# Three attention stages on one TensorE queue: the AV of one chunk and the last QK group of a later chunk moved into one slot

## The chip, the cores and the metric

One of the eight cores of a Trainium2 chip runs the kernel. The metric is the device time of one launch in microseconds, the median of several runs. Before the change it is 1178.77 us (three runs, 1178.74 to 1179.63).

Engine names as the profile has them: PE is the matrix engine (PEld its weight loads), DVE the vector engine, ACT the scalar engine, POOL GpSimd, SP the engine that only issues DMAs here.

## The reference, cut to what matters

Talking-heads attention over 4 batches, 12 heads, 448 positions, head size 64, and behind it two feed-forward stages over the 1792 tokens. All in float32.

```
scores = scale * (q @ k^T)                       # QK, per head
scores = einsum('bhij,hg->bgij', scores, w_pre)  # "pre": mixes the 12 heads
attn   = exp(scores - max) / (sum + 1e-9)
attn   = einsum('bhij,hg->bgij', attn, w_post)   # "post": mixes the heads again
x      = attn @ v                                # AV, per head
x = moe_solu(x)    # 768 -> 1024 -> 768, softmax gate and layer norm
x = moe_relu2(x)   # 768 -> 2048 -> 768, squared relu
```

## The kernel before, in words

Each batch's 448 query rows are cut into four **chunks** of 120, 120, 120 and 88 rows, sixteen chunks in all. A chunk is worked in **blocks** of up to ten query rows times twelve heads (120 partitions): twelve blocks in a chunk of 120 rows, nine in one of 88. There are 180 blocks. `ch["first"]` is a chunk's first block and `nb` its number of blocks.

The work of a chunk, in the order in which data flows:

- `qk(c, g)`, three groups g of four heads each. A group makes four PSUM tiles of 120x448; the two halves of a pair of heads lie in partitions 0 to 63 and 64 to 127 of the inputs and are issued in turn (line 199). From chunk 2 on each product is three matmuls of split numbers, so a group is 12 matmuls of 64 rows. ACT copies the four tiles to `ssrc` (line 208).
- `shuffle(t)`, a DMA on SP that regroups one block's rows with all heads into `sdst` (line 214; seven buffers).
- `pre(t)` (line 226, the full 120x120 weights), `negmax` on DVE (239), `expo` on ACT (251), `weigh` for a pair of blocks (DVE 260 and 262, then POOL 268, for the last 14 blocks ACT 275), `post(t)` (line 288), `post_out` on DVE (302).
- `av(c, p)`, six head pairs (line 315). Each is 8 products with weights of 112x64, one head in output partitions 0 to 63, the other in 64 to 127. ACT copies each tile out to `xt` (lines 325, 330). In the trace each float32 product of pre, post and AV shows as two matmuls, so a chunk's AV is 96 of them.

QK and AV tiles come from one PSUM ring, `psq_p` with tag "qa" and four buffers. After the last QK group that pool is closed and AV goes on with a ring of two (line 582).

**What sets the order.** There is no scheduler: every engine runs the program in the order in which the code issues it, and that order is a list of slots written out by hand. Slot s issues `pre(s+3)` and `post(s)`, and between them the jobs entered for that slot with `at_slot`: QK groups, splits of q and k into two parts (DVE and POOL), AV. Line 554 sets the order of the kinds inside a slot. For a chunk c behind a chunk of 12 blocks, `first` of the chunk between being F, the QK groups of c stand in slots F-8, F-4 and F; AV of chunk c-2 stands in slot F+2. The first shuffle of chunk c stands in slot F+4.

Pieces of the first feed-forward stage's weights are converted on the side: `filler` hands out one step of `narrow` (ACT line 70, DVE lines 71 to 83) at a time, about one piece per three slots up to slot 150. From slot `last_raw` (155) on, `prep_first` loads that stage's weights and inputs (`wraw`, SP lines 393 and 402; casts on DVE and ACT, line 406; POOL line 407): one step per slot up to slot `last_qk`, the slot of the last QK group, and two per slot from there (lines 584 to 588). `last_qk` is also where the QK pools are closed.

Of the kernel before, what the change touches and what calls it, by code (L numbers as in the profile page):

```python
# [18 lines left out]
def kernel(  # L19
# [69 lines left out]
    def filler():  # L89

        for q in (fill2, fill):
            while q:
                if next(q[0], None) is None:
                    q.pop(0)
                else:
                    break
# [24 lines left out]
    for b in range(B):  # L121
        for (i0, n) in CHUNKS:
            c, nb, oa = len(chunks), -(-n // R), 0
# [86 lines left out]
    def shuffle(t):  # L210
        c, k, r, oa = blocks[t]
        n, nb = chunks[c]["n"], chunks[c]["nb"]
        d = late_p.tile([120, S], F32, tag="sdst", name="sdst", bufs=7)
        nc.sync.dma_start(out=d[0:r * H], in_=ssrc[c][k:k + (r - 1) * nb + 1:nb])
        sdst[t] = d
# [6 lines left out]
    def pre(t):  # L222
        m = blocks[t][2] * H
        d = sdst.pop(t)
        ps = psb_p.tile([128, 512], F32, tag="pre", name="ps_pre", bufs=2)
        nc.tensor.matmul(  # L226
            out=ps[0:m, 0:S],
            lhsT=wpre_bd[0:m].rearrange("p i g -> p (i g)")[:, 0:m],
            rhs=d[0:m],
            start=True,  # L230
            stop=True,
        )
        pres[t] = ps

    def negmax(t):
        ps = pres[t]
        m = blocks[t][2] * H
        nm = late_p.tile([120, 1], F32, tag="nm", name="nm", bufs=4)
        nc.vector.tensor_reduce(out=nm[0:m], in_=ps[0:m, 0:S], op=ALU.max, axis=AX.X, negate=True)  # L239
        pres[t] = (ps, nm)  # L240

    def expo(t):
        m = blocks[t][2] * H
        ps, nm = pres.pop(t)
        e = late_p.tile([120, S], F32, tag="e", name="e", bufs=4)
        if t % 2 == 0:
            sms[t] = late_p.tile([120, 2], F32, tag="sm", name="sm", bufs=4)
            if m < 120 or blocks[t + 1][2] < R:
                nc.vector.memset(sms[t], 1.0)
        sm = sms[t - t % 2][:, t % 2:t % 2 + 1]  # L250
        nc.scalar.activation(  # L251
            out=e[0:m], in_=ps[0:m, 0:S], func=AF.Exp, bias=nm[0:m], scale=1.0, accum_out=sm[0:m]
        )
        es[t] = e

    def weigh(t):

        m = max(blocks[u][2] for u in (t, t + 1)) * H
        sm = sms.pop(t)
        nc.vector.tensor_scalar(out=sm[0:m], in0=sm[0:m], scalar1=1e-9, scalar2=None, op0=ALU.add)  # L260
        filler()
        nc.vector.reciprocal(sm[0:m], sm[0:m])  # L262
        filler()
        for u in (0, 1):
            m = blocks[t + u][2] * H
            w = late_p.tile([120, H, R], F32, tag="w", name="w", bufs=4)
            if t < tail:
                nc.gpsimd.tensor_tensor(  # L268
                    out=w[0:m].rearrange("p g i -> p (g i)"),
                    in0=wpost_bd[0:m].rearrange("p g i -> p (g i)"),  # L270
                    in1=sm[0:m, u:u + 1].to_broadcast([m, H * R]),
                    op=ALU.mult,
                )
            else:
                nc.scalar.activation(out=w[0:m], in_=wpost_bd[0:m], func=AF.Copy, scale=sm[0:m, u:u + 1])  # L275
            ws[t + u] = w
# [5 lines left out]
    def post(t):  # L282
        r = blocks[t][2]
        m = r * H
        e, w = es.pop(t), ws.pop(t)
        ps = psa_p.tile([JW, NJ, H, R], F32, tag="post", name="ps_post", bufs=2)
        for j in range(NJ):
            nc.tensor.matmul(  # L288
                out=ps[:, j, :, 0:r],
                lhsT=e[0:m, j * JW:(j + 1) * JW],  # L290
                rhs=w[0:m, :, 0:r],
                start=True,
                stop=True,
            )
        pps[t] = ps

    def post_out(t):
        c, k, r, oa = blocks[t]
        ps = pps.pop(t)
        if c not in at:  # L300
            at[c] = late_p.tile([JW, NJ, H, 120], F32, tag="at", name="at", bufs=2)
        nc.vector.tensor_copy(at[c][:, :, :, oa:oa + r], ps[:, :, :, 0:r])  # L302
# [109 lines left out]
    def h1(m):  # L412
        t = xs.pop(m)
        pool = psi_p if m % 2 else psh_p
        ps = pool.tile([128, 2, 512], F32, tag="h", name="ps_h")
        for cc in range(CC):
            for (a, w) in ((0, 0), (0, 1), (1, 0)):
                for u in range(2):
                    nc.tensor.matmul(  # L419
                        out=ps[:, u],  # L420
                        lhsT=t[:, a, cc],
                        rhs=w1i[cc][:, w, u * 512:(u + 1) * 512],
                        start=(cc == 0 and a == 0 and w == 0),
                        stop=(cc == CC - 1 and a == 1),
                    )
            yield True
        hps[m] = ps

    def run(part):
        for _ in part:  # L430
            pass
# [54 lines left out]
    def at_slot(s, f, *a):  # L486
        jobs.setdefault(s, []).append((f, a))

    NG = HP // KG
    splits = []  # L490
    for c, ch in enumerate(chunks):
        if c:
            p = chunks[c - 1]
            beg = ch["first"] - DS - p["nb"]
            if c > 1:
                splits += [(beg - 2, split_q, c, u) for u in (1, 0)]
            for g in range(NG):
                s = beg + (g * p["nb"]) // NG
                at_slot(s, qk, c, g)
                if c > 1 and (ch["i0"] == 0 or c == 2):  # L500
                    splits += [(s - 2, split_k, ch["b"], g, u) for u in (1, 0)]

    s = NB
    for by, f, x, *a in sorted(splits, key=lambda j: -j[0]):
        s = min(s, by - by % 2)
# [24 lines left out]
    for s in range(lo_s, NB + 12):  # L530
        js = jobs.pop(s, [])
        for kind in (load_k, load_q, load_v, load_w1, load_const):
            for f, a in js:
                if f is kind:
                    f(*a)
        if 0 <= s + DS < NB:
            shuffle(s + DS)
        for f, a in js:
            if f is store_w1:
                f(*a)  # L540
            elif f is x_out and s < NB:
                f(*a)
        if 0 <= s + DP < NB:
            pre(s + DP)
        if 0 <= s - 1 < NB:
            post_out(s - 1)
        if 0 <= s + 1 < NB and (s + 1) % 2 == 0:
            weigh(s + 1)
        else:
            filler()  # L550
        if 0 <= s + DP < NB:
            negmax(s + DP)
            expo(s + DP)
        for kind in (qk, split_q, split_k, av):
            for f, a in js:
                if f is kind:
                    f(*a)
        for f, a in js:
            if f is start_w1:
                f(*a)  # L560
        if 0 <= s < NB:
            post(s)
        filler()
        if s >= NB:
            for f, a in js:
                if f is x_out:
                    f(*a, nc.scalar)
        if s == last_raw:
            raws.__exit__(None, None, None)
            wi1 = tc.tile_pool(name="wi1", bufs=1, side="left", reuse_waits="tile")  # L570
            wi1_p = wi1.__enter__()
            prep = prep_first()
        if s == last_qk:
            early.__exit__(None, None, None)
            sspools[0].__exit__(None, None, None)
            wi1b = tc.tile_pool(name="wi1b", bufs=1, side="left", reuse_waits="tile")
            wi1b_p = wi1b.__enter__()
            psq.__exit__(None, None, None)
            psh = tc.tile_pool(name="psh", bufs=1, side="left", space=PSUM, reuse_waits="tile")
            psh_p = psh.__enter__()  # L580
            pst = tc.tile_pool(name="pst", bufs=1, side="left", space=PSUM, reuse_waits="tile")
            av_ring[:] = [pst.__enter__(), "av", 2]
            h10 = h1(0)
        if last_raw < s <= min(last_qk, last_raw + 7):
            next(prep)
        if s > last_qk:
            next(prep, None)
            next(prep, None)
        if s in (170, 172, 176, 177):
            next(h10)  # L590
        if s == NB:
            run(prep)
            run(h10)
# [388 lines left out]
```

## Time and profile before

| | |
|---|---|
| median of three runs | 1178.77 us |
| span of the profiled execution | 1178.6 us (the page gives no other time for it) |
| PE busy | 1168.5 us, 99% of the span |
| DVE, ACT, POOL busy | 744.8, 490.9, 279.8 us |
| granted PE clock | 9 of 9 in each of the 40 slices |
| attention stage | 0 to about 466 us |

A matmul's busy time in this profile overlaps that of the next, and its end is modelled. The reading used below is therefore the distance between the starts of two groups of matmuls in the timeline, which holds whatever PE did or waited for in between.

### The profile page before, as it was taken

Reading aid. Unit: us, or ns where it says so; the run is one execution under the profiler, and the core shown is the slowest. Engines: PE = TensorE matmul, PEld = TensorE weight load, DVE = VectorE, ACT = ScalarE, POOL = GpSimd, SP = SyncE. Lnnn points to the kernel's source line nnn. Section 1 sums busy time; section 2 is a strip of 40 time slices with the busy share of each in tenths; the row PEclk is TensorE's granted clock in tenths of the full one; section 3 lists DMA queues with packets and bytes.
Section 4 is the critical chain, followed back from the end, with each engine's and each line's share of the span. In section 5 each row is a group of like instructions: output and inputs, shape, how many; then the busy total and the mean of one; then the engine's idle time right before and its main releaser. Section 6 shows DMA issues by size and latency. Waiting matters only on the chain.

```text
span 1178.6 us, 21505 instructions
## 1 busy us (share of the span) xinstructions
PE 1168.5 (99%) x8034; PEld 1021.1 (87%) x8034; DVE 744.8 (63%) x1480; ACT 490.9 (42%) x1206; POOL 279.8 (24%) x386
## 2 busy tenths in 40 slices
PE   9999999999999999999999999999999999999998
PEld 4777777777777768899899999999999999999998
DVE  4776777677777664853354378457676767676734
ACT  4556555666666554422122146533232222222211
POOL 2342223223322161730110074211111111111100
PEclk9999999999999999999999999999999999999999
DMA  6875766566656452411110265212121212121113
GB/s 178 215 200 166 224 185 193 164 216 202 185 179 195 137 172 86 121 48 48 54 41 27 70 200 173 69 41 64 45 62 46 65 44 63 45 66 43 41 68 121
DMA packets 103267, 134.40 MB, mean 114 GB/s; under 512 B 21499, under 2 KB 86395, under 8 KB 103163
## 3 DMA queue, kind: packets, MB, share of 16 engines
q1 hardware_dynamic: 102379, 132.75, 37.7%
q8 instruction: 64, 1.05, 0.4%
q14 instruction: 40, 0.33, 0.1%
q10 hardware_dynamic: 784, 0.27, 0.1%
HBM read 71.65 MB, written 22.81 MB: 80 GB/s over the span
## 4 chain that ended last, share of the span: by engine, by line
PE 91%; DVE 2%; DMA 2%; ACT 1%; issue 1%; POOL 1%; SPq 0%; POOLq 0%; DVEq 0%; ACTq 0%
PE ps_y L885 19%; PE ps_h L846 19%; PE ps_post L288 12%; PE ps_pre L226 10%; PE ps_h L419 10%; PE ps_o L692 8%; PE ps_av L315 6%; PE ps_qk L199 6%; PE ps_tr L678 1%; DMA x2r<-x2D 1%; DMA wraw<-w1iD 1%; DMA wr<-in_moe_w_out_dram 1%; DVE nm L239 1%; DVE at L302 0%; ACT e L251 0%
## 5 line engine op out<-in xcount | busy, mean ns | idle before, releaser
L846 PE MATMUL ps_h<-x,ti 128*128 128x384 f32 (+1 forms) x1440 | 241.6, 325 | 0.0
L885 PE MATMUL ps_y<-to,g 128*128 128x384 f32 x1332 | 239.3, 336 | 1.1 <-ACT y L894 1.1
L846 PEld LDWEIGHTS ps_h<-x,ti 128*128 128x128 f32 x1440 | 236.6, 188 | 0.0
L885 PEld LDWEIGHTS ps_y<-to,g 128*128 128x128 f32 x1332 | 231.0, 188 | 3.4 <-DVE y L896 1.9
L288 PEld LDWEIGHTS ps_post<-w,e 120*112 120x112 f32 (+1 forms) x1440 | 168.3, 177 | 68.4 <-issue 48.2
L302 DVE COPY at<-ps_post 112x480 f32<-112x480 f32 x180 | 117.3, 652 | 109.4 <-PE ps_post L288 108.9
L288 PE MATMUL ps_post<-w,e 120*112 120x120 f32 (+1 forms) x1440 | 182.7, 270 | 2.6 <-ACT w L275 2.1
L251 ACT ACTIVATE e<-ps_pre,nm 120x448 f32<-120x448 f32 x180 | 114.6, 637 | 132.0 <-POOL w L268 73.3
L226 PE MATMUL ps_pre<-sdst,wpre_bd 120*120 120x448 f32 x360 | 166.3, 545 | 0.8 <-ACT e L251 0.7
L854 ACT ACTIVATE r<-ps_h 128x384 f32<-128x384 f32 (+1 forms) x80 | 37.4, 468 | 213.1 <-PE ps_h L846 213.1
L692 PE MATMUL ps_o<-zt,w1o 128*128 128x384 f32 (+1 forms) x720 | 120.1, 326 | 0.0
L419 PE MATMUL ps_h<-w1i,xs 128*128 128x512 f32 x504 | 119.2, 393 | 0.4 <-ACT xt L330 0.4
L855 DVE SCALAR_TENSOR_TENSOR r<-ps_h,r 128x384 f32<-128x384 f32 (+1 forms) x80 | 42.4, 531 | 121.7 <-ACT r L854 121.7
L692 PEld LDWEIGHTS ps_o<-zt,w1o 128*128 128x128 f32 x720 | 117.0, 189 | 0.0
L239 DVE TENSOR_REDUCE nm<-ps_pre 120x1 f32<-120x448 f32 x180 | 110.2, 613 | 7.9 <-PE ps_pre L226 5.3
L896 DVE TENSOR_TENSOR y<-ps_y,y 128x768 f32<-128x768 f32 x97 | 92.4, 953 | 31.2 <-PE ps_y L885 31.2
L419 PEld LDWEIGHTS ps_h<-w1i,xs 128*128 128x128 f32 x504 | 93.9, 188 | 19.9 <-ACT xt L330 0.6
L268 POOL TENSOR_TENSOR w<-wpost_bd,sm 120x120 f32<-120x120 f32 x166 | 64.1, 406 | 188.1 <-DVE sm L262 176.8
L208 ACT COPY ssrc<-ps_qk 120x448 f32<-120x448 f32 (+1 forms) x186 | 84.9, 543 | 10.0 <-PE ps_qk L199 10.0
L315 PEld LDWEIGHTS ps_av<-at,v 112*64 112x64 f32 x1536 | 73.8, 137 | 11.4 <-ACT ssrc L208 5.3
L802 POOL TENSOR_TENSOR ti<-wt,ti 128x384 fp32r<-128x384 f32 x32 | 34.7, 1085 | 205.4 <-ACT ti L801 205.3
L315 PE MATMUL ps_av<-at,v 112*64 112x120 f32 (+1 forms) x1536 | 78.0, 261 | 0.4 <-ACT xt L325 0.3
(79 smaller groups left out, 1168.1 us busy)
## 6 DMA issues: line engine op xcount, KB each, us to landing
sdst<-ssrc SPq DMA_DIRECT2D x172, 210.0 KB
wr<-in_moe_w_in_dram SPq DMA_DIRECT2D x32, 384.0 KB
wr<-in_moe_w_out_dram SPq DMA_DIRECT2D x32, 384.0 KB
w1raw<-in_moe_w_in_dram SPq DMA_DIRECT2D x24, 256.0 KB
w1raw<-in_moe_w_out_dram SPq DMA_DIRECT2D x24, 256.0 KB
kraw<-in_kT_dram SPq DMA_DIRECT2D x24, 224.0 KB
v<-in_v_dram SPq DMA_DIRECT2D x16, 336.0 KB
out_dram<-y SPq DMA_DIRECT2D x13, 384.0 KB
```

Of the source, the lines that this page charges most:

```text
L208: (nc.vector.tensor_copy if dve else nc.scalar.copy)(ssrc[c][0:n, h, :], ps[0:n, 0:S])
L226: nc.tensor.matmul(out=ps[0:m, 0:S], lhsT=wpre_bd[0:m].rearrange("p i g -> p (i g)")[:, 0:m], rhs=d[0:m], start=True, stop=True,)
L239: nc.vector.tensor_reduce(out=nm[0:m], in_=ps[0:m, 0:S], op=ALU.max, axis=AX.X, negate=True)
L251: nc.scalar.activation(out=e[0:m], in_=ps[0:m, 0:S], func=AF.Exp, bias=nm[0:m], scale=1.0, accum_out=sm[0:m])
L288: nc.tensor.matmul(out=ps[:, j, :, 0:r], lhsT=e[0:m, j * JW:(j + 1) * JW], rhs=w[0:m, :, 0:r], start=True, stop=True,)
L302: nc.vector.tensor_copy(at[c][:, :, :, oa:oa + r], ps[:, :, :, 0:r])
L315: nc.tensor.matmul(out=ps[64 * e:64 * e + 64, 0:n], lhsT=vv[ch["b"], j][:, 2 * p + e], rhs=a[:, j, 2 * p + e, 0:n], start=(j == 0), stop=( ...
L419: nc.tensor.matmul(out=ps[:, u], lhsT=t[:, a, cc], rhs=w1i[cc][:, w, u * 512:(u + 1) * 512], start=(cc == 0 and a == 0 and w == 0), stop=( ...
L692: nc.tensor.matmul(out=ps[:, 0:width], lhsT=w1o[k][:, w, cc * 128:(cc + 1) * 128], rhs=zT[:, a, k, 0:width], start=(k == 0 and i == 0), st ...
L846: nc.tensor.matmul(out=ps[:, 0:n], lhsT=ti[:, w, cc, f * 128:(f + 1) * 128], rhs=x2[q][:, a, cc], start=(cc == 0 and i == 0), stop=(cc == ...
L885: nc.tensor.matmul(out=ps[:, u - us[0], 0:DM // 2], lhsT=g[:, a, f, o:o + 128], rhs=to[:, w, f, u * (DM // 2):(u + 1) * (DM // 2)], start= ...
L896: nc.vector.tensor_tensor(out=yo, in0=po, in1=yo, op=ALU.add)
```

## The change

QK groups of chunks from 2 on move two slots later where the chunk between has 12 blocks, so from F-8, F-4, F to F-6, F-2, F+2. The last then shares slot F+2 with AV of chunk c-2, and the order of kinds inside a slot puts AV ahead of QK. Chunks behind a chunk of nine blocks (4, 8 and 12) keep their slots.

```diff
-            for g in range(NG):
-                s = beg + (g * p["nb"]) // NG
+            shift = 2 if c > 1 and p["nb"] == 12 else 0
+            for g in range(NG):
+                s = beg + shift + (g * p["nb"]) // NG
+                if shift and g == NG - 1:
+                    s = ch["first"] - p["nb"] + 2
                 at_slot(s, qk, c, g)
                 if c > 1 and (ch["i0"] == 0 or c == 2):
                     splits += [(s - 2, split_k, ch["b"], g, u) for u in (1, 0)]
...
-        for kind in (qk, split_q, split_k, av):
+        for kind in (av, qk, split_q, split_k):
```

The first place is PE's queue around block 12, where chunk 2's last QK group and chunk 0's AV stand (`ps_qk` is QK, `ps_av` AV, `ps_pre` and `ps_post` the two mixes). Before:

```order
L226 MATMUL ps_pre<-sdst,wpre_bd 120x448
L199 MATMUL ps_qk<-k,q 120x448 x12
L288 MATMUL ps_post<-w,e 112x120 x4
L226 MATMUL ps_pre<-sdst,wpre_bd 120x448
L288 MATMUL ps_post<-w,e 112x120 x4
L226 MATMUL ps_pre<-sdst,wpre_bd 120x448
L315 MATMUL ps_av<-at,v 64x120 x48
L288 MATMUL ps_post<-w,e 112x120 x4
```

And now:

```order
L288 MATMUL ps_post<-w,e 112x120 x4
L226 MATMUL ps_pre<-sdst,wpre_bd 120x448
L315 MATMUL ps_av<-at,v 64x120 x48
L199 MATMUL ps_qk<-k,q 120x448 x12
L288 MATMUL ps_post<-w,e 112x120 x4
L226 MATMUL ps_pre<-sdst,wpre_bd 120x448
```

AV and the QK group now follow each other with no post and pre between. This happens at 11 of the 16 AVs (chunks 0, 1, 3, 4, 5, 7, 8, 9, 11, 12 and 13).

The second place is SP's queue at the start (`qraw` is the load of a chunk's queries, in two halves; `sdst` a shuffle). Before:

```order
L451 DMA wp_raw<-in_w_post_dram 120x1x12
L166 DMA qraw<-in_qT_dram 64x720 x2
L214 DMA sdst<-ssrc 120x1x448 x2
L166 DMA qraw<-in_qT_dram 64x720 x2
L214 DMA sdst<-ssrc 120x1x448 x8
```

And now:

```order
L451 DMA wp_raw<-in_w_post_dram 120x1x12
L166 DMA qraw<-in_qT_dram 64x720 x4
L214 DMA sdst<-ssrc 120x1x448 x10
L434 DMA g_sb<-in_moe_g_ln_dram 128x8x1
L214 DMA sdst<-ssrc 120x1x448 x4
```

The later K splits of chunk 2 push its query load, and the split of its queries, ahead of the first two shuffles.

The third place is SP's queue around slots 161 to 165, the last QK group and behind it (`wraw` is a step of `prep_first`). Before:

```order
L393 DMA wraw<-w1iD 128x256 x2
L214 DMA sdst<-ssrc 120x1x448
L402 DMA wraw<-xD 128x2x128 x2
L214 DMA sdst<-ssrc 120x1x448
L402 DMA wraw<-xD 128x2x128
L393 DMA wraw<-w1iD 128x256
L214 DMA sdst<-ssrc 120x1x448
L340 DMA xD<-xt 128x6x120
L393 DMA wraw<-w1iD 128x256 x2
```

And now:

```order
L393 DMA wraw<-w1iD 128x256 x2
L214 DMA sdst<-ssrc 120x1x448
L402 DMA wraw<-xD 128x2x128 x2
L214 DMA sdst<-ssrc 120x1x448
L340 DMA xD<-xt 128x6x120
L402 DMA wraw<-xD 128x2x128
L393 DMA wraw<-w1iD 128x256
```

`last_qk` goes from 159 to 161, so two steps of `prep_first` fall out of slots 160 and 161 and everything behind them comes one slot later; `xD<-xt` (AV of chunk 13) stays in slot 164.

## Rows read from the trace of the kernel before

**Rows 1.** The page: busy us (share of the span) and instructions of each engine.

```profile
PE   1168.5 (99%) x8034; PEld 1021.1 (87%) x8034; DVE 744.8 (63%) x1480; ACT 490.9 (42%) x1206; POOL 279.8 (24%) x386
```

**Rows 2.** The page: the chain of waits that ended last, by engine.

```profile
PE 91%; DVE 2%; DMA 2%; ACT 1%; issue 1%; POOL 1%; SPq 0%; POOLq 0%; DVEq 0%; ACTq 0%
```

**Rows 3.** Timeline of PE around one QK group; first start us, then us.

```profile
203.99 0.92 PE L226 MATMUL ps_pre<-sdst,wpre_bd 120*120 120x448 f32 x2
204.74 0.98 PE L288 MATMUL ps_post<-w,e 120*112 120x120 f32 x8
205.56 0.92 PE L226 MATMUL ps_pre<-sdst,wpre_bd 120*120 120x448 f32 x2
206.41 1.48 PE L199 MATMUL ps_qk<-k,q 64*120 64x448 f32 x12
207.82 1.07 PE L288 MATMUL ps_post<-w,e 120*112 120x120 f32 x8
208.74 0.92 PE L226 MATMUL ps_pre<-sdst,wpre_bd 120*120 120x448 f32 x2
```

**Rows 4.** Timeline of PE around one AV.

```profile
190.86 0.92 PE L226 MATMUL ps_pre<-sdst,wpre_bd 120*120 120x448 f32 x2
191.71 5.14 PE L315 MATMUL ps_av<-at,v 112*64 112x120 f32 x96
196.78 1.07 PE L288 MATMUL ps_post<-w,e 120*112 120x120 f32 x8
```

**Rows 5.** Timeline of ACT: that AV's last copy, and a QK group's four.

```profile
196.90 0.37 ACT L325 COPY xt<-ps_av 128x120 f32<-128x120 f32 x1 [0.45 <-PE ps_av L315]
...
202.75 1.82 ACT L208 COPY ssrc<-ps_qk 120x448 f32<-120x448 f32 x4
```

**Rows 6.** Timeline of PE in slots 161 to 173, the end of attention.

```profile
412.06 1.86 PE L315 MATMUL ps_av<-at,v 112*64 112x120 f32 x32
414.18 3.50 PE L315 MATMUL ps_av<-at,v 112*64 112x120 f32 x64 [0.26 <-ACT xt L325]
417.61 1.07 PE L288 MATMUL ps_post<-w,e 120*112 120x120 f32 x8
...
430.31 1.07 PE L288 MATMUL ps_post<-w,e 120*112 120x120 f32 x8 [1.18 <-ACT w L275]
...
434.40 1.07 PE L288 MATMUL ps_post<-w,e 120*112 120x120 f32 x8 [0.61 <-ACT w L275]
...
439.53 0.67 PE L288 MATMUL ps_post<-w,e 120*112 120x120 f32 x4 [0.33 <-ACT w L275]
```

**Rows 7.** Timeline of ACT in the same stretch.

```profile
429.56 0.40 ACT L406 CAST w1i<-wraw 128x256 fp32r<-128x256 f32 x1 [1.89 <-DMA wraw<-w1iD]
```

**Rows 8.** Timeline of SP in the same stretch (SPq is its queue).

```profile
429.27 0.82 SPq L214 DMA_DIRECT2D sdst<-ssrc  x1
...
431.19 0.82 SPq L214 DMA_DIRECT2D sdst<-ssrc  x1
```

**Rows 9.** The tile ps_post: what the engines that touch it waited for (us, times).

```profile
  POOL w L268: 13.0, 36
```

**Rows 10.** Timeline of PE where such a wait is among the longest.

```profile
175.40 0.92 PE L226 MATMUL ps_pre<-sdst,wpre_bd 120*120 120x448 f32 x2
176.51 1.07 PE L288 MATMUL ps_post<-w,e 120*112 120x120 f32 x8 [0.20 <-POOL w L268]
```

**Rows 11.** Timeline of SP, then of PE, at the start.

```profile
13.75 1.73 SPq L214 DMA_DIRECT2D sdst<-ssrc  x2
15.58 1.17 SPq L166 DMA_DIRECT2D qraw<-in_qT_dram  x2
...
18.06 1.76 PE L226 MATMUL ps_pre<-sdst,wpre_bd 120*120 120x448 f32 x4
```

## The prediction, made before the changed kernel ran

> **What bounds the kernel now.** I read the busy shares first: PE is busy for 1168.5 of 1178.6 us, and no other engine for more than 63% [rows 1]. The chain of waits agrees, 91% of it PE [rows 2]. So the time is what PE's queue takes, and a change of order can gain only where it shortens PE's own distances or takes a wait out of the few that are there. Next I read the timeline of PE around one QK group, and took distances from start to start [rows 3]. Between two posts a pre takes 204.74 - 203.99 = 0.75 us, and a post between two pres 205.56 - 204.74 = 0.82. Ahead of QK the same pre takes 206.41 - 205.56 = 0.85, and behind QK the same post 208.74 - 207.82 = 0.92. Nothing is marked as waited for there; the two 0.10 us belong to going from one kind of matmul to the other. QK is issued with 64 rows, pre and post with the full 120. AV, 64 columns wide, pays the same at its entry: 191.71 - 190.86 = 0.85 [rows 4]. Each visit to QK or AV so costs about 0.19 us beyond its own matmuls (0.20 by these rows, whose last digit is rounded; I take 0.19).
>
> **The change, part by part.**
>
> *The shared slot.* At 11 places QK follows AV directly. One long pre and one long post per place go back to their short form: 11 x 0.19 = 2.1 us less. Pre, post, QK and AV keep their number. What I can't see is the step from AV to QK, which does not occur before. The nearest rows are the two steps that do: out of AV into post (inside the 196.78 - 191.71 = 5.07 us of AV) and from pre into QK (inside QK's 207.82 - 206.41 = 1.41 us) [rows 3, 4]. If leaving AV for QK costs what leaving AV for post costs, and entering QK costs what it costs behind pre, the saving stays at 2.1. If the step were free at both ends, as much again could go as a visit's two long neighbours cost, another 0.19 per place or 2.1 in all; if it cost double, the whole 2.1 is lost. I take the middle, since both halves stand in rows.
>
> The Trainium skill, "TensorEngine Tiling (Array Packing)", Key Properties, says that changing the tiling mode, not merely the tile, drains the engine. That is what the 0.10 us on either side of QK look like. AV and QK use different modes by that rule, so it is for the middle value: a shared slot has three changes of mode where two separate ones have four.
>
> *What stands behind AV.* QK's four PSUM tiles now come out of the ring of four right behind AV's six. QK's first pair needs the tiles of AV's third and fourth head pair, long copied; its second pair those of the fifth and sixth. ACT's last AV copy starts at 196.90 and takes 0.37, so it ends 0.49 us after AV's end at 196.78 [rows 4, 5]. QK's second pair starts about half of 1.41, 0.70 us, behind its first. The wait is hidden with 0.2 us to spare; without that cover it would cost what the copy is late. I charge 0.1 in all, bounds 0 and 4.1 (one copy of 0.37 at each of 11 places). ACT then copies QK's four tiles in 1.82 us [rows 5], while PE has post and pre of two slots, about 3.1 us, before it needs ACT again. The shuffle of the chunk's first block stands two slots behind the QK group instead of four; that block's pre comes seven slots, some 11 us, behind the group. I charge nothing; if that cover went, the price would be one wait at 11 places.
>
> The same page of the Trainium skill warns under "PSUM Bottleneck" that tiling speeds up TensorE but not the evacuation, so ten tiles in a row through four buffers ought to end in ACT. The row is against it here: an AV head pair takes PE 5.07 / 6 = 0.85 us and ACT 0.37.
>
> *The weights' lateness in mid-stage.* A post waits where POOL has not made its weights; the view of `ps_post` counts 36 such waits, 13.0 us on the weight loads [rows 9], most of it hidden on PE. A visible case: pre takes 176.51 - 175.40 = 1.11 instead of 0.75 in slot 64, the slot ahead of a QK group [rows 10]. DVE and POOL fall behind where four slots pass with neither QK nor AV, and in half of the chunks the pair's first post stands at the end of such a stretch. Before, the stretches go 4, 4, 2, 2 slots; now 4, 4, 4, with one long pause of 6.5 us. So in five or six chunks one more stretch ends in such a wait, while the ones that coincided with K splits move off them. I take +0.4, bounds -0.6 (half of the visible ones gone) and +2.2 (six more of 0.36).
>
> *The end of attention.* AV of chunk 13 took 417.61 - 412.06 = 5.55 us instead of 5.07, as its third tile waited for a copy in the ring of two [rows 6]. Now `last_qk` is its own slot, and it still draws on the ring of four: -0.5, bounds 0 and -0.5. Behind it post waits three times for ACT's weights, 1.18 + 0.61 + 0.33 = 2.1 us [rows 6], because ACT stands at a cast of `wraw` that had not landed [rows 7], and SP needs 431.19 - 429.27 = 1.92 us for a shuffle and two loads where PE takes 0.75 + 0.82 = 1.57 for a slot [rows 3, 8]. Now two more loads (0.9 us by that row's pace) come behind the long slot, but each is due one slot, 1.57 us, later, and the last of the three waits falls into the slot of the next AV, which hides it. I take -0.5, bounds -2.1 (all gone) and +0.9 (the two loads late and nothing hidden).
>
> *The start.* SP issues chunk 2's queries (1.17 us) ahead of the first shuffle [rows 11]. They may start once QK of chunk 0 has read the buffer, shortly before 13.75, so the shuffle goes out up to 0.5 us later; its pre starts at 18.06, 4.3 us after the issue, directly behind QK matmuls. I charge 0, bounds 0 and +0.5. From 466 us on nothing is reordered.
>
> **The sum.** -2.1 + 0.1 + 0.4 - 0.5 - 0.5 = -2.6 us on the profiled span of 1178.6, that is 1176.0. The median of the runs lies 0.17 above that span; with it 1176.2. I forecast **1176.1 us**, 0.23% faster. About 0.2%, 2.4 us, is what a measurement of this kernel tells from no change, so the forecast lies on that edge.
>
> **Rivals.**
> - *The waits eat it.* The step gains 2.1, but the longer stretches without QK cost their upper bound of 2.2 and the end of attention gains nothing but the 0.5: about 1178.3, no change. For it: DVE's and POOL's lateness already shows. Against: the visible cases need weight pieces, and these end by slot 150.
> - *The step from AV to QK is free.* Then 2.1 more go: 1174.0. For it: the weights of QK could load while AV's last columns pass. Against: QK's first matmuls behind pre do not.
> - *Slower: the ring.* AV's last copy, behind exp and five others in ACT's queue, is not done when QK's second pair starts. From 0.2 us of lateness on PE waits; one copy late at 11 places is 4.1 us: 1176.1 + 4.1 = 1180.2. For it: ten tiles pass through four buffers in one slot, and the AV with a ring of two did wait [rows 6]. Against: the 0.49 us above.
> - *It doesn't do what it says.* The long pre and post come from something else than the neighbour, as from a semaphore that PE must look at, and stay: only the end of attention moves, 1178.
>
> **How the numbers follow.** Forecast (1175 to 1177.4) 0.56, free step 0.10, eaten waits 0.20, no such saving 0.08, slower by the ring 0.06. Faster by more than 0.2% means below 1176.4: some three quarters of the forecast's share, the free step, and a little of the eaten waits, 0.58 in all. Slower by more than 0.2% is the ring's share, 0.06; the rest, 0.36, is within. The range from 1174.2 to 1178.2 takes in the free step's and the eaten waits' times and leaves out about 2 in 10.
>
> **What would show it.** Right: in PE's timeline QK starts 5.0 to 5.1 us behind AV's start, QK takes 1.4 there, and pre and post around the former place of the last group read 0.75 and 0.82; AV of chunk 13 reads 5.07; the three waits for ACT's weights add up to less than 2.1 us. Wrong: a wait for ACT's copies inside QK at the shared slots, more waits for POOL's weights, or AV's end drawn out ahead of QK by more than it is ahead of post.

## The result and the profile after

The changed kernel takes 1193.17 us (median of six runs, 1189.26 to 1197.04) against 1179.33 us for the kernel before on the same chip (six runs, 1178.74 to 1180.57): a ratio of 1.0119, 95% interval 1.0101 to 1.0138. It is 1.2% slower where 0.2% faster was forecast. The profiled execution is the longest of the six, 1195.2 us of span.

The page of the changed kernel: busy us of the engines, the granted PE clock in 40 slices (9 is 0.9 of the full clock or more), and the chain by engine, against [rows 1, 2].

```profile
PE 1175.6 (98%) x8034; PEld 1026.2 (86%) x8034; DVE 748.3 (63%) x1480; ACT 493.7 (41%) x1206; POOL 280.9 (24%) x386
...
PEclk9989999999999999999999999999999999999999
...
PE 93%; DMA 2%; DVE 2%; ACT 1%; issue 1%; POOL 0%; SPq 0%; POOLq 0%; DVEq 0%; ACTq 0%
```

At this distance almost nothing is to be seen: the chain is still PE's, the shares are the same. The one new sign is an 8 in the clock's third slice. The whole difference lies in the attention stage: its last post starts 16.1 us later than before, the rest of the span takes the same within 0.5 us.

**What came as forecast.** PE's timeline around a shared slot (start us, then us), beside [rows 3, 4]:

```profile
201.19 5.14 PE L315 MATMUL ps_av<-at,v 112*64 112x120 f32 x96
206.26 1.45 PE L199 MATMUL ps_qk<-k,q 64*88 64x448 f32 x12
207.64 1.07 PE L288 MATMUL ps_post<-w,e 120*112 120x120 f32 x8
208.55 0.92 PE L226 MATMUL ps_pre<-sdst,wpre_bd 120*120 120x448 f32 x2
209.31 0.98 PE L288 MATMUL ps_post<-w,e 120*112 120x120 f32 x8
```

QK starts 206.26 - 201.19 = 5.07 us behind AV, as post did before; it takes 1.38 and waits for no copy. At all eleven places QK takes 1.38 to 1.41. AV takes the 5.07 too, but for the first place, where it waits for its values (below), and for the three AVs of 88 rows (3.79 to 4.12). With 11 pres and 11 posts back in their short form, PE's distances give about 11 x 0.185 = 2.0 us less (a long pre and post against a short pair, read with three decimals). AV of chunk 13 reads 5.07 where it read 5.55 [rows 6].

**What nobody had counted on.** DVE's timeline in slots 15 to 18; in brackets, how long the engine stood before the instruction, and whose end released it:

```profile
62.10 0.61 DVE L239 TENSOR_REDUCE nm<-ps_pre 120x1 f32<-120x448 f32 x1
66.19 0.40 DVE L157 CAST k<-kraw 128x448 fp32r<-128x448 f32 x1 [3.48 <-PE ps_qk L199]
66.50 0.65 DVE L302 COPY at<-ps_post 112x480 f32<-112x480 f32 x1
67.07 0.76 DVE L260 TENSOR_SCALAR sm<-sm 120x2 f32<-120x2 f32 x1
67.86 0.17 DVE L262 RECIPROCAL sm<-sm 120x2 f32<-120x2 f32 x1
```

POOL in the same stretch:

```profile
66.67 1.14 POOL L158 TENSOR_TENSOR k<-kraw,k 128x448 fp32r<-128x448 f32 x1 [5.33 <-DVE k L157]
68.20 0.79 POOL L268 TENSOR_TENSOR w<-wpost_bd,sm 120x120 f32<-120x120 f32 x2 [0.39 <-DVE sm L262]
```

And PE:

```profile
64.67 1.46 PE L199 MATMUL ps_qk<-k,q 64*88 64x448 f32 x12
68.64 1.94 PE L288 MATMUL ps_post<-w,e 120*112 120x120 f32 x8 [2.51 <-POOL w L268]
70.37 1.70 PE L226 MATMUL ps_pre<-sdst,wpre_bd 120*120 120x448 f32 x2
71.86 1.81 PE L288 MATMUL ps_post<-w,e 120*112 120x120 f32 x8
73.46 1.69 PE L226 MATMUL ps_pre<-sdst,wpre_bd 120*120 120x448 f32 x2
74.96 1.02 PE L288 MATMUL ps_post<-w,e 120*112 120x120 f32 x8
```

Read from the bottom up: post stands 2.51 us for POOL's weights; POOL had them late because DVE's `weigh` (lines 260, 262) was late; `weigh` stood in DVE's queue behind the K cast; and the cast waited 3.48 us for a QK group. The cast writes the K tile of the *next* batch into the buffer that the last chunk of *this* batch still reads: one tile per group (tag `k{g}`), one buffer. QK(3, 0), its last reader, went from slot 16 to 18; the cast stayed in slot 16. The view of line 157 gives three such waits in the whole run, one for each change of batch:

```profile
its engine sat idle before it (us, times) until:
  PE ps_qk L199: 9.3, 3
```

The kernel before already stood at the edge: its view of the same line lists two short waits, at the first and the third change of batch, where reader and writer stood in the same slot. This is the view, and the first of the two on DVE:

```profile
  PE ps_qk L199: 0.5, 2
```

```profile
61.13 0.39 DVE L157 CAST k<-kraw 128x448 fp32r<-128x448 f32 x1 [0.26 <-PE ps_qk L199]
```

The second thing stands in the same rows of PE. Behind the wait the distances are double: a pre takes 71.86 - 70.37 = 1.49 instead of 0.75 us, a post 73.46 - 71.86 = 1.60 instead of 0.82. The view of stretches of time (us; busy us and number of instructions by engine; then the granted PE clock, DMA share, GB/s):

```profile
64.00:68.20 4.20, 2.12 (x14) 0.86 (x13) 1.97 (x5) 0.00 (x0) 1.14 (x2) 1.00 0.92 249
68.20:75.00 6.80, 6.36 (x21) 4.65 (x22) 5.21 (x13) 4.21 (x11) 2.77 (x5) 0.50 0.48 137
75.00:80.00 5.00, 5.00 (x36) 3.42 (x35) 4.81 (x13) 1.80 (x6) 1.76 (x3) 1.00 0.41 142
```

For some 6.8 us the granted clock is 0.50, the lower of the two levels (1.2 and 2.4 GHz). It falls while PE stands for the weights. Two more such stretches, 3.4 us each, follow the waits at 295 and 443 us. Before, the clock was 1.0 from 3.8 us to the end. The spread of its six runs goes with it: the run of 1189.3 us has a mean clock of 0.999, those of 1196 and 1197 us have 0.993 and 0.994. A mean of 0.006 less is 7 us more here, which is about the difference. But the run at 0.999 is still 9.9 us above the kernel before, so the clock is the smaller part of the loss.

Three waits are not of this chain. AV of chunk 0 waits for a value load:

```profile
52.25 2.99 PE L315 MATMUL ps_av<-at,v 112*64 112x120 f32 x54 [1.84 <-DMA v<-in_v_dram]
```

Ahead of slots 57 and 58 DVE stands for a piece of the feed-forward weights, with its later work for pre and post queued behind. The pres and posts of these two slots take 1.4 us longer than before. Why that piece landed late was not read; e1 and e3 below show no such loss there.

```profile
158.73 0.29 DVE L71 TENSOR_SCALAR w1t<-w1raw 128x256 uint32<-128x256 uint32 x1 [1.48 <-DMA w1raw<-in_moe_w_in_dram]
```

At the end of attention one post waits 2.17 us, because ACT stands at a cast for an input load with its weights behind it; in [rows 6] the three waits there were 1.18, 0.61 and 0.33:

```profile
445.45 0.40 ACT L406 CAST xs<-wraw 128x256 fp32r<-128x256 f32 x1 [2.88 <-DMA wraw<-xD]
445.76 0.68 ACT L275 ACTIVATE w<-wpost_bd,sm 120x120 f32<-120x120 f32 x2
```

The view of `ps_post`, where [rows 9] had 13.0 us in 36 waits:

```profile
  POOL w L268: 31.2, 51
```

**The account**, from PE's distances between the first post and post 165, against the kernel before:

| | us |
|---|---|
| long pres and posts at 11 places gone | -2.0 |
| posts 18 and 108 late behind QK | +5.1 |
| pres and posts stretched in the two stretches at clock 0.50 | +4.8 |
| other late pres and posts (slots 64 to 66, at the second change of batch: 1.9; slots 57 and 58: 1.4; slot 70: 0.8) | +5.2 |
| AV (chunk 0 +1.9; chunk 13 -0.5, the rest small) | +1.7 |
| sum | +14.8 |

The end of attention adds 1.2 (mainly the third stretch, 1.7, and the wait at post 168, 1.0 more, with two later waits of 1.3 in sum gone), the start 0.1.

### The profile page after: what moved, and what is told of

Its sections match the earlier page's. It is cut to its first block, busy times and chain, and to the rows that moved or that the text cites. A ratio compares the mean times of both kernels' runs of the same rounds, so it can differ in the third digit from the quotient of the medians.

```text
span 1195.2 us, 21495 instructions
## 1 busy us (share of the span) xinstructions
PE 1175.6 (98%) x8034; PEld 1026.2 (86%) x8034; DVE 748.3 (63%) x1480; ACT 493.7 (41%) x1206; POOL 280.9 (24%) x386
## 4 chain that ended last, share of the span: by engine, by line
PE 93%; DMA 2%; DVE 2%; ACT 1%; issue 1%; POOL 0%; SPq 0%; POOLq 0%; DVEq 0%; ACTq 0%
PE ps_h L849 19%; PE ps_y L888 19%; PE ps_post L288 12%; PE ps_pre L226 10%; PE ps_o L695 10%; PE ps_h L419 10%; PE ps_av L315 6%; PE ps_qk L199 6%; PE ps_tr L681 1%; DMA v<-in_v_dram 1%; PE ps_pre L444 1%; ACT e L251 1%; DMA wraw<-xD 0%; DVE at L302 0%; DVE nm L239 0%
## 5 line engine op out<-in xcount | busy, mean ns | idle before, releaser
L288 PEld LDWEIGHTS ps_post<-w,e 120*112 120x112 f32 (+1 forms) x1440 | 172.3, 180 | 81.2 <-issue 51.1
L288 PE MATMUL ps_post<-w,e 120*112 120x120 f32 (+1 forms) x1440 | 185.5, 273 | 9.1 <-POOL w L268 6.9
L226 PE MATMUL ps_pre<-sdst,wpre_bd 120*120 120x448 f32 x360 | 169.7, 555 | 2.0 <-ACT e L251 1.7
```

What stands on the lines that cost most here:

```text
L226: nc.tensor.matmul(out=ps[0:m, 0:S], lhsT=wpre_bd[0:m].rearrange("p i g -> p (i g)")[:, 0:m], rhs=d[0:m], start=True, stop=True,)
L288: nc.tensor.matmul(out=ps[:, j, :, 0:r], lhsT=e[0:m, j * JW:(j + 1) * JW], rhs=w[0:m, :, 0:r], start=True, stop=True,)
```

## The experiments

The theory (A): a writer of a K buffer was left ahead of its moved reader, and the clock's drops hang on the waits that this makes. The rival (B): ten tiles and their ten copies in one slot are too many, and the cast's wait is a symptom.

**e1: the K split behind its reader.** Where a K split and a query split come due at the same slot, the query split now goes first.

```diff
-    for by, f, x, *a in sorted(splits, key=lambda j: -j[0]):
+    for by, f, x, *a in sorted(splits, key=lambda j: (-j[0], j[1] is split_q)):
```

> Changed kernel, one edit: where a K split and a query split come due at the same slot, the K split takes the later slots (20, 22 for chunk 4, group 0; 66, 68; 110, 112) and the query split the earlier. The order of TensorE and ScalarE stays. Theory A (buffer): in the changed kernel VectorE stood 3.48, 2.31 and 3.47 us at the K cast of the next batch, because the last chunk of a batch reads that K buffer and its first QK group had moved to two slots later, behind the cast; weights queued behind the cast came late and TensorE stood at posts 18, 64, 66 and 108 (about +2.6, +3.0, +2.6 us), and two of three stretches at granted clock 0.5 followed (about +3.1 and +1.7 us). So those casts wait under 0.3 us, the stretches at 68 and 300 us are gone, and the time falls by 10 to 13 us to about 1180 (1179 to 1183); AV of chunk 0 (7.1 us) and the wait at post 168 stay. Rival B (crowding): the post waits come from the QK group's four copies and the AV's six copies that now lie in one slot; the casts' wait is only a symptom. Then posts 18, 64, 108 stay late and the time stays at 1189 or more.

Measured: 1179.33 us (1178.43 to 1180.40), ratio to the kernel before 0.9997, interval 0.9988 to 1.0006. DVE, then PE, at the same place:

```profile
67.53 0.62 DVE L239 TENSOR_REDUCE nm<-ps_pre 120x1 f32<-120x448 f32 x1
68.08 0.38 DVE L157 CAST k<-kraw 128x448 fp32r<-128x448 f32 x1
```

```profile
62.71 1.46 PE L199 MATMUL ps_qk<-k,q 64*88 64x448 f32 x12
64.09 1.07 PE L288 MATMUL ps_post<-w,e 120*112 120x120 f32 x8
65.01 0.92 PE L226 MATMUL ps_pre<-sdst,wpre_bd 120*120 120x448 f32 x2
```

No cast waits, post comes 1.38 us behind QK, the clock is 1.0 throughout. One line takes back 13.8 us, with PE's and ACT's order untouched; theory B, crowding, has fallen. Not all of it is the cast. AV of chunk 0, which was expected to stay at 7.1, reads 5.07: the K loads moved with the split, from ahead of the last value load to behind it. At the end the distances ahead of posts 168 and 170 are 1.1 us too long each, 2.3 in sum (2.6 at three posts before the change), with no drop of the clock behind them.

**e2: the same line in the kernel before.**

> Control: the kernel before with the same single edit of the splits' order (K split of group 0 on the later slots, query split on the earlier). Theory A: nothing there waited for a K buffer, so the time is that of before within 0.2% (1177 to 1181 us). Rival B says the same, so it is a control on e1: were it faster or slower by several us, e1's difference would come from the splits' places themselves.

Measured: 1178.44 us, ratio 0.9993, interval 0.9984 to 1.0003. No difference that can be told. So e1's gain is not the worth of the new order as such; it is the waits, the cast's above all and, for 2.1 us of the trace, AV's for its values.

**e3: three of the 33 moved QK groups alone.** On the kernel before:

```diff
-                s = beg + (g * p["nb"]) // NG
+                s = beg + (g * p["nb"]) // NG + (2 if g == 0 and c % 4 == 3 and c < 15 else 0)
```

> One part of the change alone, on the kernel before: only the first QK group of the last chunk of batches 0 to 2 (chunks 3, 7, 11) is two slots later (slots 18, 63, 108 in place of 16, 61, 106); the other 30 moved groups, the AVs and the order within a slot stay. Theory A (buffer): these three alone bring the K casts' waits of 2 to 3.5 us, late weights at posts 18, 64 to 66 and 108 and the stretches at granted clock 0.5 behind them: 1187 to 1193 us. Rival B (crowding): no group shares its slot with an AV, so nothing is crowded: 1178 to 1180 us.

Measured: 1189.27 us (1186.97 to 1190.27), ratio 1.0084, interval 1.0071 to 1.0098. Line 157's view reads as in the changed kernel, `PE ps_qk L199: 9.3, 3`, and so does PE:

```profile
63.95 1.45 PE L199 MATMUL ps_qk<-k,q 64*88 64x448 f32 x12
67.91 1.94 PE L288 MATMUL ps_post<-w,e 120*112 120x120 f32 x8 [2.50 <-POOL w L268]
69.64 1.64 PE L226 MATMUL ps_pre<-sdst,wpre_bd 120*120 120x448 f32 x2
71.11 0.98 PE L288 MATMUL ps_post<-w,e 120*112 120x120 f32 x8
```

Three groups out of 33, none of them in a shared slot, bring 9.9 of the 13.8 us (in the profiled run 1.2 of it is AV of chunk 0, which waits for its values here too). Its profiled run has one stretch at clock 0.50 (67.7 to 71.1 us) where the changed kernel's had three; its wait at 290 us, 2.51 us long, drew none.

**e4 and e11: the mended kernel.** e1, with the value loads of batch 0 two slots earlier and the old pace of `prep_first`; run twice, the second time beside e10.

```diff
-[6, 8, 10, 12] if c == 0 else [0, 2, 4, 6]
+[4, 6, 8, 10] if c == 0 else [0, 2, 4, 6]
...
-        if last_raw < s <= min(last_qk, last_raw + 7):
+        if last_raw < s <= last_qk - 2:
             next(prep)
-        if s > last_qk:
+        if s > last_qk - 2:
```

> Changed kernel with three edits: the K split's order of e1; the value loads of batch 0 two slots earlier (4, 6, 8, 10); the first weights of the last stage prepared at the old pace (single steps to slot 159, two from slot 160). Theory A: beside e1's 10 to 13 us, AV of chunk 0 falls from 7.1 to about 5.1 us (2 us) and the wait at post 168 (2.2 us with 1.7 us at granted clock 0.5 behind it) goes back to that of before: 1175 to 1178 us, the saving of the shared slots of about 2 us now seen below before. Rival C (no net gain): shared slots make small waits at other posts (three to four us in sum) that eat their 2 us: 1178 to 1180. Rival B: 1187 or more.

> The mended kernel once more, to stand beside e10 on the same chip: 1178 to 1179.2 us by every theory.

Measured: 1178.57 us (ratio 0.9997, 0.9988 to 1.0006) and 1178.75 us (0.9994, 0.9986 to 1.0003). Rival C: no gain that can be told. The two further edits bring nothing over e1 that can be told either. Up to post 165 the trace of e4 is 1.4 us ahead of the kernel before: -2.0 for the shared slots, -0.4 in AV, -0.1 in QK, and +1.1 in small waits of pre and post. The view of `ps_post` points the same way, 15.8 us against the 13.0 of [rows 9]:

```profile
  POOL w L268: 15.8, 42
```

At the end another 0.8 goes, on posts that wait 1.75 and 0.88 us for ACT's weights. In the profiled run of e11, the same kernel, the first of them comes 2.4 us late and a stretch at clock 0.50 follows.

**e8: QK ahead of AV.** The mended kernel with the other order inside the slot.

```diff
-        for kind in (av, qk, split_q, split_k):
+        for kind in (qk, av, split_q, split_k):
```

> The mended kernel with QK before AV in a shared slot. If AV first matters (its ring of four buffers and its copies on ScalarE free QK's way early, and the QK copies come last), QK first makes AV's first pairs wait for the QK group's copies and the exp behind them later: AV over 5.2 us at 11 places, 1179 to 1182 us. If it doesn't, AV stays at 5.07 us and the time is that of the mended kernel within 0.1%.

Measured: 1194.29 us (ratio 1.0135, 1.0118 to 1.0153), 15.7 over the mended kernel where at most 3.4 were expected. PE, then ACT, at a shared slot:

```profile
79.76 1.45 PE L199 MATMUL ps_qk<-k,q 64*88 64x448 f32 x12
82.69 5.14 PE L315 MATMUL ps_av<-at,v 112*64 112x120 f32 x96 [1.48 <-ACT ssrc L208]
```

```profile
81.50 0.63 ACT L251 ACTIVATE e<-ps_pre,nm 120x448 f32<-120x448 f32 x1 [0.35 <-DVE nm L239]
82.03 0.19 ACT L251 ACTIVATION_READ_ACCUMULATOR e<-ps_pre,nm 120x1 f32 x1
82.12 1.81 ACT L208 COPY ssrc<-ps_qk 88x448 f32<-88x448 f32 x4
```

AV's first tile needs a buffer of the ring that QK's copies have not left; and ACT starts these copies only behind the exp of the slot's own pre, at 82.12. QK to AV takes 2.93 us instead of 1.38; AV itself keeps its 5.07, so the wait stands ahead of it and not inside, where it was expected. Over the eleven places the extra distance of QK adds up to 14.9 us, nearly all of the 15.7. The ring of four is a real limit; AV first, whose last copies are done in time, is what keeps it off PE. AV came 0.8 to 2.0 us late eleven times, and the clock stayed at 1.0.

**e6 and e7: the query casts on ACT.** e6 on the mended kernel, e7 on e2.

```diff
-        nc.vector.tensor_copy(hi, r)
+        nc.scalar.copy(hi, r)
```

> The mended kernel (K split late, value loads early, old preparing pace; 1178.6 us) with one more edit: the first half of each query split (the cast, 0.33 us) goes from VectorE to ScalarE. Its trace has late posts after slots with a query cast (slots 45 and 46, 57, 64 to 66, 78, 136 and 147: about 3 us in sum, each on POOL's weights or ScalarE's exp). Theory D (VectorE's backlog): a separate QK or AV slot gave VectorE a break every four slots or so; where the two share one slot there are eight or nine plain slots in a row, VectorE is full there and falls behind, and weights come late. Without the casts these waits fall to a third, 1.5 to 2.5 us less: 1176 to 1177.3. Theory E (ScalarE's backlog): the ten copies of a shared slot delay exp behind them; then a cast more on ScalarE makes it the same or slower: 1178.5 to 1180.5.

> Control for e6: the kernel before with the K split's late order (1178.4 us) and the query cast on ScalarE. Theory D: its waits in mid-stage are shorter (about 2 us in sum), so at most 1 us is gained: 1177.3 to 1178.5; then e6 should lie under it by about 1 us, the part of the shared slots' 2 us that was eaten. Theory E: 1178.4 or up to 1 us more.

Measured: 1195.97 us (1.0136, 1.0118 to 1.0155) and 1192.74 us (1.0113, 1.0098 to 1.0128). Both theories missed by far. POOL, then ACT, then PE, in e6:

```profile
111.51 0.95 POOL L176 TENSOR_TENSOR q<-qraw,q 128x360 fp32r<-128x360 f32 x1 [4.39 <-ACT q L175]
112.42 0.91 POOL L268 TENSOR_TENSOR w<-wpost_bd,sm 120x120 f32<-120x120 f32 x2
```

```profile
109.22 1.82 ACT L208 COPY ssrc<-ps_qk 120x448 f32<-120x448 f32 x4
110.90 0.53 ACT L175 CAST q<-qraw 128x360 fp32r<-128x360 f32 x1
```

```profile
113.04 1.39 PE L288 MATMUL ps_post<-w,e 120*112 120x120 f32 x8 [2.52 <-POOL w L268]
```

It is the same mistake in another queue: the cast stands behind QK's four copies on ACT, POOL's subtract waits for it, and the weights stand behind the subtract. It says nothing of DVE's load. Theory D's premise was also wrong: by the list of slots a QK group follows two or four slots behind every shared one but the last, so until there at most three plain slots stand in a row, not eight or nine.

**e9: a slower pace of `prep_first`**, on e6: from slot 160 one step in even slots, two in odd ones.

```diff
             next(prep, None)
-            next(prep, None)
+            if s % 2:
+                next(prep, None)
```

> e6 with a slower pace of the preparing of the last stage's first weights: from slot 160 one step in an even slot and two in an odd one, in place of two in every slot. In the mended kernel's trace ScalarE stands 2.46, 0.63, 1.19 us at casts that wait for a weight's DMA, with the weights of the last 14 blocks queued behind, and posts 168, 170 wait 1.91 and 1.13 us. Theory: a load now has 3.3 slots in place of 2.5 until its cast, so these waits go under 1 us in sum: 2 us less than e6, so 1174.5 to 1176. Rival: the later end of the preparing is missed by the matmuls behind the attention stage, and nothing is gained or 1 us is lost.

Measured: 1196.68 us (1194.27 to 1197.01; ratio to the kernel before 1.0142, 1.0126 to 1.0157), no faster than e6. Post still waits 1.0 us for ACT's weights, and a pre now stands 0.9 us for its shuffle. No gain, as the rival had it.

**e10: the query splits into the shared slots**, on the mended kernel, with the casts on DVE.

```diff
-            if c > 1:
+            if c > 2 and p["first"] - chunks[c - 2]["first"] == 12:
+                sq = p["first"] - 12 + 2
+                at_slot(sq, split_q, c, 0)
+                at_slot(sq, split_q, c, 1)
+                at_slot(sq - 6, load_q, c)
+            elif c > 1:
                 splits += [(beg - 2, split_q, c, u) for u in (1, 0)]
```

> The mended kernel with both query splits of a chunk (casts on VectorE, subtracts on GpSimd, as ever) moved into the slot that AV and a QK group share, behind both (slots 14, 26, 47, 59, 71 and so on), in place of two even slots among the plain ones. e6 did not test theory D: on ScalarE the cast stood behind the slot's copies, GpSimd's subtract waited for it with the weights behind it. Theory D (VectorE's backlog in the long plain stretches): the waits of the mended kernel at slots 45 and 46, 57, 78, 136 and 147 (0.3 to 0.9 us each, about 2.5 us in sum) go to under 1 us in sum: 1176 to 1177.5. Rival F (the weights' and exp's lateness comes from the shared slot's own copies or the weights' narrowing, not from the casts): the waits stay, 1178 to 1179.5; and if the four operations in one slot hold up GpSimd's weights there, 1179.5 to 1182.

Measured: 1179.51 us (1176.83 to 1183.23; ratio 1.0006, 0.9995 to 1.0017), e11 beside it 1178.75. Against e4's trace the extra distance at slot 46 goes from 0.4 to 0.2 us and at slot 144 from 0.5 to 0.2, but those at 82 and 148 (0.4 each) stay, and in slots 66 to 71 some 2.6 us more are lost behind a late weight of POOL (1.5 us), 1.7 of it in a stretch at clock 0.50. Inconclusive: in these two traces a part of the small waits goes with the casts, not most of them. Where the rest of the 1.1 us comes from stays open.

## Why the prediction was wrong

*The shared slot* (-2.1): right, -2.0. The step from AV to QK costs what was assumed, so the rival of a free step is out, and so is the one by which the change doesn't do what it says.

The support that the prediction gave its middle value does not carry it, though: one change of mode less in four would, at an equal price each, be a quarter of the 0.38 us of two visits, 1.0 us at 11 places and not 2.1. What went is the price of two; no row shows a price for the new step, as AV takes 5.07 and QK 1.40 there as elsewhere.

*What stands behind AV* (+0.1): right for the order that the change has, with no wait for AV's copies at any of the eleven places. e8 shows that the ring would have decided in the other order.

*The weights' lateness in mid-stage* (+0.4, at most +2.2): **this is the step that failed.** It said that weights which had coincided with K splits "move off them", and took a split as so much work for DVE and POOL. A split is also the writer of a tile that an earlier QK group reads, from a single buffer. In the kernel before the two stood in one slot, 16, the reader first; the change moved the reader to 18 and left the writer. Neither the bounds nor a rival had a wait of DVE for QK, though the trace of before showed one at this very cast: 0.26 us at 61.13, with the reader in the writer's own slot. Two slots more for the reader had to lengthen it. e3 makes this loss with those three groups alone, e1 takes it away by moving the writers. With the wait away this step measures +1.1 in the account of e4, inside its bounds, and much in the way that was forecast: six slots (46, 70, 82, 136, 144, 148) lose 2.9 us in sum and four (56, 64, 68, 146) gain 1.8.

*The clock.* The sum took every distance at the full granted clock, as the page of before shows it. With waits above 2 us on PE that no longer held, and two stretches at half clock made 4.8 of the 14.8 us.

*The end of attention* (-0.5 and -0.5): AV of chunk 13 gained its 0.5. Of the three waits two went, but the first grew from 1.18 to 2.17 us, and the third stretch at half clock stands behind it: +1.2 in all. In e1, with the same pace of `prep_first`, the lateness there is again about what it was in sum (2.3 against 2.6 us), so the pace alone does not make it; what does was not settled.

*The start* (0, at most +0.5): first post at 24.06 us against 23.93, right. AV of chunk 0 was not in the sum at all. It now comes ahead of the QK group that used to precede it, so it needs its values earlier; the wait was 1.84 us in the changed kernel, but e3, with that AV in its old place, shows 1.2 us more than before there too, and e1, with the K loads behind the last value load, none. So the order of the loads matters at least as much as AV's place.

*The range and small slips.* The range from 1174.2 to 1178.2 was said to take in the free step's and the eaten waits' times; they are 1174.0 and 1178.3, just outside. The two loads on SP take 1.92 - 0.82 = 1.1 us by the row, not 0.9, and the sum ends at 1176.2, not 1176.1. None of this bears on a miss of 17 us.

*What remained*: had the writers moved along, the forecast would still have been 2 us too good. The mended kernel lies 0.4 to 0.8 us below the kernel before in two comparisons that can't tell it from no change, where 2.6 were forecast; no version here is faster by more than can be told.

## What to carry to other kernels

When a reader is moved later in a hand-written order, look up the next writer of each of its buffers, not only the data that it needs: with one buffer the writer turns into a wait, and what is queued behind the writer pays. A short wait of the writer for the reader in the trace of before, here 0.26 us, shows that there is no room. The same holds for moving work to an idle engine: e6 moved a cast of 0.33 us from the busier DVE to ACT, where it stood behind four copies, and lost 17 us by what waited for it. And a wait of 2.5 us on PE may cost more than 2.5: behind most such waits here the clock halved and the work of the next 3.4 us took twice its time.

## What the hardware showed that was not expected

PE's granted clock falls to 0.50 in mid-kernel, on an engine that is busy 98% of the span. In the profiled runs of the changed kernel and of all the experiments, 11 of the 12 places where a post came 2.2 to 2.7 us late show a stretch at 0.50 that begins in the wait or within 1.5 us behind it. Of 9 places late by 1.5 to 1.9 us one does (e10). Of the AVs that came late, none does: e8's eleven, by 0.8 to 2.0 us, and AV of chunk 0, by 2.1 in the changed kernel and 1.4 in e3. Each stretch measured 3.4 us, one 6.8, and cost half its length, as the doubled distances show. In e1, e2, e4 and e8, where no post came more than 2 us late, the clock is 1.0 throughout. The drops do not hang on the K casts: in e6, e7 and e9 the posts come late by the query casts on ACT, and all six places of 2.3 to 2.7 us show one. That the length of the wait alone decides is not shown, since no run varied it with all else equal.
